# A short first tile, its own score buffers, filler transposes and new planned transfer times in a planned attention stage

## The chip, the cores and the metric

One core of a Trainium2 chip runs the whole program. The metric is the device time of one execution in microseconds (us). Five engines work side by side and meet at semaphores: TensorE (PE in the rows; PEld is its weight load), VectorE (DVE), ScalarE (ACT), GpSimd (POOL) and SyncE (SP), which here only issues DMAs. Transfers issued from SP and POOL are carried by the same 16 DMA engines; the rows call their busy time the DMA share.

## The reference

Three layers follow one another. The first is attention with mixed heads, for 4 batches, 12 heads, 448 positions and a head size of 64:

```python
scores = scale * np.matmul(q, k.transpose(0, 1, 3, 2))
scores = np.einsum('bhij,hg->bgij', scores, w_pre)
attn = np.exp(scores - np.max(scores, axis=-1, keepdims=True))
attn = attn / (np.sum(attn, axis=-1, keepdims=True) + 1e-09)
attn = np.einsum('bhij,hg->bgij', attn, w_post)
return np.matmul(attn, v)
```

Its output, 1792 tokens of 768, goes through a layer h = x @ w_in, h * cos(h), @ w_out (inner width 2048), and that through a soft mixture of 8 experts. w_in and w_out come as doubles (float64) and are turned to float32 by the kernel itself.

## The kernel before, in words

**Stages.** phase_a is the attention (to about 533 us), phase_b the middle layer (to about 850 us), phase_c the experts. Only phase_a is touched.

**Tiles and groups.** Each batch's 448 query rows are cut into four tiles, t = 0 to 3, of 120, 120, 120 and 90 rows (ROWS); in a 90-row tile 88 rows are new and two are loaded twice. The 16 tiles stand in the list `tiles`, batch by batch and t = 0, 1, 2, 3. A tile is worked off in groups of 30 rows: 4 groups, or 3 for t = 3 (NG), 60 in all. `gi` counts groups and `ti` tiles.

**Steps of a tile.**
- load_q (L253) loads its queries into qnat in three parts of four heads, each one DMA, or two for t = 3 (80 rows and 10 rows). load_k (L239) loads a batch's keys in two halves of four DMAs; load_v (L271) its values in three.
- k_prep (L283) and q_prep (L306) transpose them on TensorE into PSUM and split each into a high and a low part (kp, kr and qh, ql) on ScalarE and VectorE. There is one qh and one ql, so q_prep of a tile waits for the scores of the tile before.
- scores (L339) makes the scores of a pair of heads in six matmuls (L351). Each head is copied out (`out`, helper lines L223 for VectorE and L225 for ScalarE) to a buffer ss from the ring "ssrc" of 8 places, and a DMA, `sort` (L366), writes it to s2, where the 12 heads of one position stand in neighbouring partitions. The sort goes from SP's queue or POOL's. A place of the ring is free again when its sort has landed.
- pre (L393) mixes heads for a third of a group: a matmul with kron_pre, the maximum on VectorE (L396), the exponential on ScalarE (L400). It needs all 12 sorts of its tile. fin (L416 to L418) forms the weights wc, post (L431) mixes again, four quarters of three matmuls each, and copies the result into am[ti % 2], one of two buffers of [112, 12, 4, 120]. av (L455) multiplies with the values, and the result is stored.

**Doubles.** `narrow` (L493) turns 64 units of 128 x 384 doubles to float32: a load raw (SP), two ScalarE steps (L507, L511), four on VectorE (L515, L519, L524, L528), two on POOL (L532, L535), a store (L538).

**The order is planned.** Every step is an Op of a Plan, with a planned duration for each engine that may do it, dependencies, a due time counted in groups, and the buffers that it takes or uses. `Plan.schedule` plays the program through with these durations and at each turn takes, among the steps that could start first on an engine, the one that is due first. Its result is the fixed order of each engine's instructions; on the chip nothing is chosen again. A transfer is planned with the issuing engine's time and with `moves`, its time on the one planned wire, after which 3.5 us (SP) or 4.5 us (POOL) pass until it counts as seen, and `late` more for some. `behind` holds a step back until another has begun. The due times of a tile count back from its first group: scores S_DUE to S_DUE + S_SPAN before it, loads before these. The units of doubles are due evenly from group N_FIRST to N_LAST, their loads 1.5 groups sooner and behind the first pre product (`mixed`) of group int(due - 3).

PSUM has 8 banks: three of tag "ps", and in the first 24 takings also banks of the tags "pre" and "post" (SPARE), which have no other use at the start.

The costs of the plan that the change touches:

```python
kload[b, half, t] = dma(0.55, 0.8, start, due=due, ...
vload[b, c] = dma(0.35, 1.3, start, due=due, late=5.0, ...
    moves=0.85, behind=[sorted_[ti, 0]] if h else [])
ld = dma(0.4, 1.0, load, due=due - 1.5, late=6.0, takes=[raws], behind=behind)
```

Of the kernel before, what the change touches and what calls it, by code (L numbers as in the profile page):

```python
# [9 lines left out]
F32 = mybir.dt.float32  # L10
# [15 lines left out]
SPARE = 3 * ["ps", "pre", "ps", "pre", "ps", "post", "pre", "post"]  # L26

K_DUE, S_DUE, S_SPAN, P_DUE, AV_DUE, AV_SPAN, STAY = 4.0, 3.2, 3.6, 1.8, 0.7, 3.0, 0.4
N_FIRST, N_LAST = 3.5, 55.0
INV2PI = 1.0 / (2.0 * math.pi)  # L30

LEAST = 3.4332275390625e-05
# [144 lines left out]
def phase_a(tc, ident, q, k, v, w_pre, w_post, xT_d, wide, start_next):  # L177
    nc = tc.nc
    B, H, S, D = q.shape
# [6 lines left out]
    with ExitStack() as ctx:  # L186
# [23 lines left out]
        ql = sp.tile([128, H // 2, 120], F32R, name="q_lo")  # L210
        am = [sl.tile([CJ, H, NJ, 120], F32, name=f"am{i}") for i in range(2)]

        tiles = [(b, t) for b in range(B) for t in range(4)]
        groups = [(ti, g) for ti, (b, t) in enumerate(tiles) for g in range(NG[t])]
        NT, NGR = len(tiles), len(groups)
        first = [groups.index((ti, 0)) for ti in range(NT)]
# [15 lines left out]
        def dma(dur, moves, start, **kw):  # L232
            return plan.op([("SP", dur)], lambda e: start(), moves=moves, **kw)
# [5 lines left out]
        def load_k(b, half, t, due, behind):  # L239
            if t == 0:  # L240
                kslot[b, half] = Slot("knat")

            def start():
                if t == 0:
                    knat[b, half] = room(sp, "knat", [CJ, NJ, 6, D], F32, f"knat{b}_{half}")
                nc.sync.dma_start(
                    out=knat[b, half][:, t],
                    in_=k[b, 6 * half:6 * half + 6, t::NJ, :].rearrange("h p d -> p h d"))
            kload[b, half, t] = dma(0.55, 0.8, start, due=due, late=3.0 if b else 0.0, takes=[] if t else [kslot[b, half]],
                                    uses=[kslot[b, half]] if t else [],  # L250
                                    behind=behind + ([kload[b, half, 0]] if t else []))

        def load_q(ti, part, due, behind):  # L253
            b, t = tiles[ti]
            m = H // 3
            if part == 0:
                qslot[ti] = Slot("qnat")

            def start():
                if part == 0:  # L260
                    qnat[ti] = room(sp, "qnat", [120, H, D], F32, f"qnat{ti}")
                h = m * part
                for r, n, i in ((0, 80, 360), (80, 10, S - 10)) if t == 3 else ((0, 120, 120 * t),):
                    nc.sync.dma_start(
                        out=qnat[ti][r:r + n, h:h + m],
                        in_=q[b, h:h + m, i:i + n, :].rearrange("h i d -> i h d"))
            qload[ti, part] = dma(1.0 if t == 3 else 0.5, 0.55, start, due=due, late=3.0 if ti > 1 else 0.0, takes=[qslot[ti]] if part == 0 else [],
                                  uses=[] if part == 0 else [qslot[ti]],
                                  behind=behind + ([qload[ti, 0]] if part else []))

        def load_v(b, c, due, behind):  # L271
            def start():
                nc.sync.dma_start(
                    out=vt[:, 4 * c:4 * c + 4],
                    in_=v[b, 4 * c:4 * c + 4].rearrange("h (p t) d -> p h t d", t=NJ))
            vload[b, c] = dma(0.35, 1.3, start, due=due, late=5.0,
                              deps=[avs[4 * b - 1, c]] if b else [], behind=behind)


# [26 lines left out]
        def q_prep(ti, x, due):  # L306
            n = ROWS[tiles[ti][1]]
            s = Slot("ps")
            cs = slice(2 * x, 2 * x + 2)

            def src():
                return made["qt", ti, x][:, :240].rearrange("p (c i) -> p c i", c=2)[:, :, :n].rearrange(
                    "p c (a i) -> p c a i", i=10)

            def dst(to):

                return to[:, cs, :n].rearrange("p c (i a) -> p c a i", i=10)

            def turn(e):
                pt = made["qt", ti, x] = bank(s, f"qt{ti}_{x}")  # L320
                for c in range(2):
                    nc.tensor.transpose(
                        pt[:, c * 120:c * 120 + n],
                        qnat[ti][:n, 4 * x + 2 * c:4 * x + 2 * c + 2].rearrange("p h d -> p (h d)"),
                        ident[:n, :n])

            def high(e):
                copy(e, dst(qh), src())

            def low(e):  # L330
                nc.vector.tensor_tensor(out=dst(ql), in0=src(), in1=dst(qh).bitcast(F32), op=ALU.subtract)
            free = [qk[ti - 1, p] for p in (2 * x, 2 * x + 1)] if ti else []
            a = plan.op([("PE", 0.21)], turn, [qload[ti, x]] + free, due, takes=[s], uses=[qslot[ti]])
            h = plan.op([("ACT", 0.32), ("DVE", 0.5)], high, [a], due, uses=[s])
            qdone[ti, x] = plan.op([("DVE", 0.5)], low, [h], due, uses=[s])
# [3 lines left out]
        def scores(ti, p, due):  # L339
# [13 lines left out]

            def out(o):
                def f(e):
                    x[o] = room(sg, "ssrc", [120, S], F32, f"ss{ti}_{2 * p + o}")
                    copy(e, x[o][:n], made["s", ti, p][o][:n, :S])
                return f

# [8 lines left out]
            qk[ti, p] = plan.op([("PE", 0.8)], mul, [kdone[b, p], qdone[ti, p // 2]], due, takes=s, half=True)  # L368
            for o in range(2):
                h = 2 * p + o  # L370
                ss = Slot("ssrc")
                if h == 0:
                    s2l[ti] = Slot("s2")
                c = plan.op(EV, out(o), [qk[ti, p]], due, takes=[ss], uses=[s[o]])
                sorted_[ti, h] = plan.op([("SP", 1.0), ("POOL", 0.8)], sort(o), [c], due,
                                         takes=[] if h else [s2l[ti]], uses=[ss] + ([s2l[ti]] if h else []),
                                         moves=0.85, behind=[sorted_[ti, 0]] if h else [])


        el, et, mz, prt, wct, expd, wcl, mixed = {}, {}, {}, {}, {}, {}, {}, {}  # L380
# [43 lines left out]
        def post(gi, jt, f, due):  # L424
# [10 lines left out]
            def out(e):  # L435
# [1 line left out]
                     made["po", gi, jt][:, :360].rearrange("p (g i) -> p g i", i=30))  # L437
            m = plan.op([("PE", 0.63)], mul, [f], due, takes=[b], uses=[el[gi], wcl[gi]])
            amdone[gi, jt] = plan.op([("ACT", 0.36), ("DVE", 0.46)], out,
                                     [m] + ([avs[ti - 2, s] for s in range(3)] if ti > 1 else []), due, uses=[b])  # L440


        xst, xl = {}, {}
# [29 lines left out]
        def av(ti, due):  # L473
# [10 lines left out]
                outs.append(plan.op([("ACT", 0.28), ("DVE", 0.36)], lambda e, s=s: av_out(ti, s, e),  # L484
                                    [avs[ti, s]], d, uses=[sl_, xl[ti]]))
            if ti < NT - 2:
                dma(0.4, 1.25, lambda: store_x(ti, nc.sync), late=5.0, deps=outs, due=due + 2, uses=[xl[ti]])


        UP = 384  # L490
# [2 lines left out]
        def narrow(u, due, behind):  # L493
# [42 lines left out]

            def store():
                nc.sync.dma_start(out=dst[:, c0:c0 + UP], in_=x["f"])  # L538
            ld = dma(0.4, 1.0, load, due=due - 1.5, late=6.0, takes=[raws], behind=behind)
            m = plan.op([("ACT", 0.46)], size, [ld], due, takes=[ms], uses=[raws])  # L540
            f = plan.op([("ACT", 0.46)], rest, [ld], due, takes=[fs], uses=[raws])
            t = plan.op([("DVE", 0.42)], bits, [ld], due, takes=[ts], uses=[raws])
# [2 lines left out]
            p = plan.op([("DVE", 0.34)], power, [t], due, uses=[ts, ms])  # L545
            f = plan.op([("POOL", 1.05)], times, [p, f], due, uses=[fs, ms])
            f = plan.op([("POOL", 1.05)], plus, [f], due, uses=[fs, ts])
            dma(0.35, 0.55, store, late=6.0, deps=[f], due=due + 1, uses=[fs])


        for b in range(B):
            for ti in range(4 * b, 4 * b + 4):
                g0, n = first[ti], NG[tiles[ti][1]]
                mark = [qk[ti - 1, 0]] if ti > 2 else [qk[1, 5]] if ti > 1 else [kload[0, 1, 3]] if ti else []
                for p in range(6):
                    d = g0 - S_DUE - S_SPAN * (5 - p) / 5
                    if p % 2 == 0:
# [653 lines left out]
```

## Time and profile before

| what | us |
|---|---|
| median of 3 runs | 962.73 |
| lowest and highest of the 3 | 960.71, 968.0 |
| the profiled execution's own time | 964.6 |
| its span, from the first to the last instruction | 962.8 |
| TensorE busy in the span | 908.4 (94%) |
| VectorE, ScalarE, GpSimd busy | 658.8, 562.3, 198.4 |
| mean granted TensorE clock | 0.972 |

The profile is one execution. A group of rows tells busy time and idle time by line of the kernel; "idle before" names the event that ended an engine's wait, inferred from semaphores, so that a name may stand for another that came at the same time. PEclk is the granted clock of TensorE, 1.00 being 2.4 GHz and 0.50 being 1.2 GHz.

### The profile page before, as it was taken

To read this page: it belongs to the slowest core of one execution; us is meant where nothing else is said; L and a number is where in the kernel's file an instruction comes from. 1 tells how busy PE (TensorE), PEld (TensorE's weight loads), DVE (VectorE), ACT (ScalarE), POOL (GpSimd) and SP (SyncE) were. 2 spreads that over 40 slices of the span, in tenths; PEclk is the share of its full clock that TensorE was granted. 3 is DMA by queue.
4 is the path that set the end of the run, shared out by engine and by line. 5 is a ranking of instruction groups with operands and counts; after the bars stand their busy time and mean duration, and the time that the engine had idled before them with its cause. 6 is when DMAs were issued, how large, how long until landed. Compare 5 with 4: busy or idle time off the path is not lost.

```text
span 962.8 us, 18155 instructions
## 1 busy us (share of the span) xinstructions
PE 908.4 (94%) x6694; PEld 650.0 (68%) x6694; DVE 658.8 (68%) x1295; ACT 562.3 (58%) x1240; POOL 198.4 (21%) x246
## 2 busy tenths in 40 slices
PE   5888999999989999998999999999999999999985
PEld 3556677676767667766778877877777778844422
DVE  4578988979879789889854756666767667833303
ACT  4566776777767758766665645556657557720102
POOL 2144443524534245334410000000000000000000
PEclk9789999999999989999999999999999999999897
DMA  9989678996678985978427731254554438899999
GB/s 178 213 182 232 181 202 209 209 250 201 169 187 206 234 217 152 231 213 209 141 65 243 255 123 50 82 197 131 181 171 157 132 115 279 262 348 380 373 372 329
DMA packets 195246, 198.92 MB, mean 207 GB/s; under 512 B 71042, under 2 KB 164368, under 8 KB 195158
## 3 DMA queue, kind: packets, MB, share of 16 engines
q1 hardware_dynamic: 184626, 176.06, 62.5%
q0 software_dynamic: 7920, 21.05, 9.2%
q8 instruction: 53, 0.87, 0.4%
q10 hardware_dynamic: 2612, 0.65, 0.3%
q14 instruction: 35, 0.29, 0.1%
HBM read 135.40 MB, written 23.59 MB: 165 GB/s over the span
## 4 chain that ended last, share of the span: by engine, by line
PE 75%; DVE 9%; DMA 9%; ACT 3%; issue 2%; SPq 1%; POOL 0%; DVEq 0%; ACTq 0%
PE po L431 13%; PE pre L393 12%; PE h L698 8%; PE h L699 8%; PE h L701 8%; PE s L351 6%; PE av L455 6%; DMA early<-in_moe_w_dram 4%; DMA s<-ss 3%; PE gt L738 3%; DVE cvt L519 2%; PE lg L747 1%; PE eh L1018 1%; PE p L810 1%; DMA qnat<-in_q_dram 1%
## 5 line engine op out<-in xcount | busy, mean ns | idle before, releaser
L431 PEld LDWEIGHTS po<-wc,e 120*112 120x112 f32 x1440 | 174.8, 180 | 71.3 <-issue 45.5
L431 PE MATMUL po<-wc,e 120*112 120x120 f32 x1440 | 187.5, 272 | 7.0 <-ACT am L225 3.3
L393 PE MATMUL pre<-s,kron_pre 120*120 120x448 f32 x360 | 173.4, 567 | 9.0 <-DMA w<-nar 3.2
L698 PE MATMUL h<-x,wh 128*128 128x512 f32 (+1 forms) x384 | 142.1, 380 | 0.0
L400 ACT ACTIVATE e<-pre,mz 120x448 f32<-120x448 f32 x180 | 115.0, 639 | 43.3 <-DVE mz L396 42.9
L396 DVE TENSOR_REDUCE mz<-pre 120x1 f32<-120x448 f32 x180 | 111.0, 620 | 40.2 <-PE pre L393 39.6
L699 PE MATMUL h<-x,wh 128*128 128x512 f32 (+1 forms) x384 | 136.3, 365 | 0.0
L225 ACT COPY am<-po 112x360 f32<-112x360 f32 x191 | 87.4, 462 | 66.6 <-PE po L431 65.1
L366 POOL DMA_DIRECT2D s<-ss x104 | 63.5, 611 | 205.7 <-ACT ss L225 148.2
L714 ACT ACTIVATE cg<-h,consts 128x512 f32<-128x512 f32 (+1 forms) x64 | 40.4, 632 | 90.8 <-PE h L701 88.0
L698 PEld LDWEIGHTS h<-x,wh 128*128 128x128 f32 x384 | 72.3, 188 | 22.9 <-ACT cg L714 8.4
L701 PE MATMUL h<-x,wf 128*128 128x512 f32 (+1 forms) x384 | 87.5, 364 | 0.0
L455 PE MATMUL av<-am,v 112*64 112x120 f32 (+1 forms) x1536 | 83.5, 265 | 0.6 <-ACT ss L225 0.5
L455 PEld LDWEIGHTS av<-am,v 112*64 112x64 f32 x1536 | 74.9, 138 | 12.4 <-issue 3.4
L532 POOL TENSOR_TENSOR nar<-nar,cvm 128x384 f32<-128x384 f32 x64 | 64.4, 1006 | 88.5 <-DVE cvm L528 32.3
L715 DVE TENSOR_SCALAR cg<-cg 128x512 f32<-128x512 f32 (+1 forms) x64 | 25.2, 394 | 79.8 <-ACT cg L714 79.4
L699 PEld LDWEIGHTS h<-x,wh 128*128 128x128 f32 x384 | 72.4, 189 | 10.5
L1024 POOL MEMSET hz<- 128x256 f32 x2 | 0.6, 305 | 358.3 <-DVE rz L973 358.3
L701 PEld LDWEIGHTS h<-x,wf 128*128 128x128 f32 x384 | 66.3, 188 | 11.8
L225 ACT COPY ss<-s 120x448 f32<-120x448 f32 (+1 forms) x109 | 56.8, 534 | 28.2 <-PE s L351 18.1
L535 POOL TENSOR_TENSOR nar<-nar,cvt 128x384 f32<-128x384 f32 x64 | 68.4, 1068 | 4.2
L393 PEld LDWEIGHTS pre<-s,kron_pre 120*120 120x120 f32 x360 | 54.0, 190 | 22.0 <-issue 19.6
(178 smaller groups left out, 1468.2 us busy)
## 6 DMA issues: line engine op xcount, KB each, us to landing
early<-in_moe_w_dram SPq DMA_DIRECT2D x36, 768.0 KB
wf<-w SPq DMA_DIRECT2D x64, 384.0 KB
s<-ss POOLq DMA_DIRECT2D x79, 210.0 KB, 6.2
s<-ss SPq DMA_DIRECT2D x65, 210.0 KB
raw<-in_moe_w_in_dram SPq DMA_DIRECT2D x32, 384.0 KB
w<-nar SPq DMA_DIRECT2D x64, 192.0 KB
raw<-in_moe_w_out_dram SPq DMA_DIRECT2D x32, 384.0 KB
gn<-in_moe_w_dram SPq DMA_DIRECT2D x16, 768.0 KB
```

The costliest lines, as they stand in the source:

```text
L225: nc.scalar.copy(out=out, in_=in_)
L366: QUEUE[e].dma_start(out=s2t[ti][h::12, :n // 10], in_=x[o][:n])
L393: nc.tensor.matmul(prt[gi, c][:, :S], kpre, s2t[ti][:, 3 * g + c, :], start=True, stop=True)
L396: nc.vector.tensor_reduce(out=mz[gi][:, 0, c:c + 1], in_=prt[gi, c][:, :S], axis=AX.X, op=ALU.max, negate=True)
L400: nc.scalar.activation(out=et[gi][:, c, :], in_=prt.pop((gi, c))[:, :S], func=AF.Exp, bias=mz[gi][:, 0, c:c + 1], accum_out=mz[gi][:, 1, c ...
L431: nc.tensor.matmul(pt[:, :360].rearrange("p (g i) -> p g i", i=30)[:, :, 10 * c:10 * c + 10], et[gi][:, c, jt * CJ:(jt + 1) * CJ], wct[gi] ...
L455: nc.tensor.matmul(pt[64 * o:64 * o + 64, x * 120:x * 120 + n], vt[:, g, jt, :], am[ti % 2][:, g, jt, :n], start=(jt == 0), stop=(jt == NJ ...
L532: nc.gpsimd.tensor_tensor(out=x["f"], in0=x["f"], in1=x["m"], op=ALU.mult)
L535: nc.gpsimd.tensor_tensor(out=x["f"], in0=x["f"], in1=x["t"].bitcast(F32), op=ALU.add)
L698: nc.tensor.matmul(pt, wh[:, c], xh[:, c, :], start=(c == 0), stop=False)
L699: nc.tensor.matmul(pt, wh[:, c], xl[:, c, :], start=False, stop=False)
L701: nc.tensor.matmul(pt, wl[:, c], xh[:, c, :], start=False, stop=(c == 5))
```

## The change

Batch 0's tiles run in the order t = 3, 0, 1, 2, so that tile 0 has 90 rows and three groups, and all groups of batch 0 after it are numbered accordingly. Tile 0's twelve score copies go to twelve places cut from am[1], which tile 1's results use first, and take no place in the ring; tile 1's results wait for tile 0's sorts. The query turns of tile 1 are each preceded by 10, 8 and 8 transposes of the identity into an unused part of their bank. Tile 1's queries are loaded behind tile 0's third pair of scores, not behind the last key load. N_FIRST is 5.5, not 3.5. The planned times of most transfers are longer: a sort's `moves` 1.0 (0.75 for 90 rows) for 0.85, a key load's 0.9 for 0.8, a query part's 0.65 for 0.55, a value load's 1.9 for 1.3, a result's store 1.5 for 1.25, the load and the store of a unit of doubles 1.45 and 0.75 for 1.0 and 0.55.

```diff
-N_FIRST, N_LAST = 3.5, 55.0
+WARM = 10, 8, 8
+N_FIRST, N_LAST = 5.5, 55.0
...
-        tiles = [(b, t) for b in range(B) for t in range(4)]
+        tiles = [(b, t) for b in range(B) for t in ((3, 0, 1, 2) if b == 0 else (0, 1, 2, 3))]
...
-            kload[b, half, t] = dma(0.55, 0.8, start, due=due, late=3.0 if b else 0.0, takes=[] if t else [kslot[b, half]],
+            kload[b, half, t] = dma(0.55, 0.9, start, due=due, late=3.0 if b else 0.0, takes=[] if t else [kslot[b, half]],
...
-            qload[ti, part] = dma(1.0 if t == 3 else 0.5, 0.55, start, due=due, late=3.0 if ti > 1 else 0.0, takes=[qslot[ti]] if part == 0 else [],
+            qload[ti, part] = dma(1.0 if t == 3 else 0.5, 0.65, start, due=due, late=3.0 if ti > 1 else 0.0, takes=[qslot[ti]] if part == 0 else [],
...
-            vload[b, c] = dma(0.35, 1.3, start, due=due, late=5.0,
+            vload[b, c] = dma(0.55, 1.9, start, due=due, late=5.0,
...
             def turn(e):
                 pt = made["qt", ti, x] = bank(s, f"qt{ti}_{x}")
+                for _ in range(idle):
+                    nc.tensor.transpose(pt[:, 256:384], ident, ident)
...
             free = [qk[ti - 1, p] for p in (2 * x, 2 * x + 1)] if ti else []
+            idle = WARM[x] if ti == 1 else 0
...
             def out(o):
-                    x[o] = room(sg, "ssrc", [120, S], F32, f"ss{ti}_{2 * p + o}")
+                    if ti:
+                        x[o] = room(sg, "ssrc", [120, S], F32, f"ss{ti}_{2 * p + o}")
+                    else:
+                        c = S * (2 * p + o)
+                        x[o] = am[1].rearrange("p h t i -> p (h t i)")[:, c:c + S]
                     copy(e, x[o][:n], made["s", ti, p][o][:n, :S])
...
             qk[ti, p] = plan.op([("PE", 0.8)], mul, [kdone[b, p], qdone[ti, p // 2]], due, takes=s, half=True)
                 h = 2 * p + o
-                ss = Slot("ssrc")
+                ss = [Slot("ssrc")] if ti else []
                     s2l[ti] = Slot("s2")
-                c = plan.op(EV, out(o), [qk[ti, p]], due, takes=[ss], uses=[s[o]])
+                c = plan.op(EV, out(o), [qk[ti, p]], due, takes=ss, uses=[s[o]])
-                                         takes=[] if h else [s2l[ti]], uses=[ss] + ([s2l[ti]] if h else []),
-                                         moves=0.85, behind=[sorted_[ti, 0]] if h else [])
+                                         takes=[] if h else [s2l[ti]], uses=ss + ([s2l[ti]] if h else []),
+                                         moves=1.0 * n / 120, behind=[sorted_[ti, 0]] if h else [])
...
             m = plan.op([("PE", 0.63)], mul, [f], due, takes=[b], uses=[el[gi], wcl[gi]])
-                                     [m] + ([avs[ti - 2, s] for s in range(3)] if ti > 1 else []), due, uses=[b])
+                                     [m] + ([avs[ti - 2, s] for s in range(3)] if ti > 1 else [sorted_[0, h] for h in range(H)] if ti else []), due, uses=[b])
...
-                dma(0.4, 1.25, lambda: store_x(ti, nc.sync), late=5.0, deps=outs, due=due + 2, uses=[xl[ti]])
+                dma(0.4, 1.5, lambda: store_x(ti, nc.sync), late=5.0, deps=outs, due=due + 2, uses=[xl[ti]])
...
-            ld = dma(0.4, 1.0, load, due=due - 1.5, late=6.0, takes=[raws], behind=behind)
+            ld = dma(0.45, 1.45, load, due=due - 1.5, late=6.0, takes=[raws], behind=behind)
...
-            dma(0.35, 0.55, store, late=6.0, deps=[f], due=due + 1, uses=[fs])
+            dma(0.4, 0.75, store, late=6.0, deps=[f], due=due + 1, uses=[fs])
-                mark = [qk[ti - 1, 0]] if ti > 2 else [qk[1, 5]] if ti > 1 else [kload[0, 1, 3]] if ti else []
+                mark = [qk[ti - 1, 0]] if ti > 2 else [qk[1, 5]] if ti > 1 else [qk[0, 2]] if ti else []
```

## Rows read from the trace of the kernel before

**Rows 1.** Stages: window, us, busy by engine (instructions), granted clock, DMA share, GB/s.
```profile
0.00:100.00 100.00, 80.80 (x490) 52.79 (x492) 63.55 (x134) 58.07 (x142) 31.13 (x46) 0.90 0.93 204
100.00:490.00 390.00, 375.45 (x3158) 273.74 (x3154) 332.94 (x666) 273.01 (x703) 164.42 (x191) 0.98 0.77 198
...
533.00:850.00 317.00, 315.44 (x1857) 246.04 (x1856) 210.99 (x392) 193.60 (x310) 0.00 (x0) 1.00 0.52 166
```

**Rows 2.** The same view of the start; busy are PE, PEld, DVE, ACT, POOL.
```profile
0.00:30.90 30.90, 17.82 (x96) 11.74 (x96) 11.13 (x23) 13.32 (x26) 7.22 (x17) 0.86 0.88 179
30.90:36.20 5.30, 5.30 (x9) 2.46 (x9) 2.45 (x5) 1.79 (x5) 0.58 (x1) 0.52 0.73 176
36.20:57.30 21.10, 17.59 (x110) 12.14 (x108) 15.66 (x37) 15.45 (x40) 5.36 (x6) 0.98 1.07 244
57.30:64.00 6.70, 6.65 (x16) 2.92 (x18) 3.05 (x6) 2.68 (x7) 0.62 (x1) 0.55 0.56 107
64.00:92.20 28.20, 25.69 (x208) 18.09 (x206) 25.36 (x53) 19.82 (x51) 14.69 (x18) 1.00 1.01 223
```

**Rows 3.** Timeline of the start: start, us, engine, line, operation [idle before, releaser].
```profile
12.03 0.72 POOL L366 DMA_DIRECT2D s<-ss  x1 [10.72 <-ACT ss L225]
...
21.42 0.62 DVE L223 COPY ss<-s 120x448 f32<-120x448 f32 x1 [3.19 <-DMA s<-ss]
21.60 0.58 POOL L366 DMA_DIRECT2D s<-ss  x1 [1.83 <-ACT ss L225]
...
25.20 0.66 PE L322 MATMUL qt<-ident,qnat 120*128 120x120 f32 x2 [6.05 <-ACT ss L225]
...
30.92 0.47 PEld L393 LDWEIGHTS pre<-s,kron_pre 120*120 120x120 f32 x2 [0.56 <-DMA s<-ss]
```

**Rows 4.** Windows of the idle stretch and of what follows it.
```profile
19.20:25.20 6.00, 0.00 (x1) 0.00 (x1) 0.62 (x1) 1.12 (x3) 1.15 (x2) 0.76 0.91 180
25.20:30.90 5.70, 4.17 (x14) 2.14 (x14) 1.48 (x3) 1.68 (x4) 1.74 (x3) 0.50 0.72 182
```

**Rows 5.** Timeline where tiles 1 and 2 open, and a late sort of tile 1.
```profile
46.77 0.58 POOL L366 DMA_DIRECT2D s<-ss  x1 [5.26 <-ACT ss L225]
...
57.35 1.82 PE L393 MATMUL pre<-s,kron_pre 120*120 120x448 f32 x2 [3.15 <-DMA w<-nar]
...
92.26 0.98 PE L393 MATMUL pre<-s,kron_pre 120*120 120x448 f32 x2 [1.95 <-DMA s<-ss]
```

**Rows 6.** DMA issues, 100 to 490 us: count, size, median us to landing.
```profile
s<-ss POOLq DMA_DIRECT2D x57, 210.0 KB, 6.1
...
s<-ss POOLq DMA_DIRECT2D x21, 157.5 KB, 3.6
```

**Rows 7.** Timeline of TensorE: twelve key transposes in a row.
```profile
12.80 1.37 PE L289 MATMUL kt<-ident,knat 112*128 112x112 f32 x12
```

**Rows 8.** Windows of the score products alone (L351): PE, PEld busy.
```profile
0.00:19.20 19.20, 7.47 (x48) 5.03 (x48) 1.00 0.91 178
```

**Rows 9.** Chain of waits: one third of a group's pre, one quarter of its post.
```profile
42.20 0.75 PE pre L393 x2
42.95 0.61 PE po L431 x6
```

**Rows 10.** VectorE's conversion groups, 100 to 490 us; last: least, median, longest ns.
```profile
L519 DVE SCALAR_TENSOR_TENSOR cvt<-raw,cvt 128x384 uint32<-128x384 uint32 x56 | 49.1, 877 | 1.0
...
L524 DVE SCALAR_TENSOR_TENSOR cvt<-cvm,cvt 128x384 f32<-128x384 f32 x56 | 35.9, 641 | 1.7 <-ACT cvm L507 0.5
...
L515 DVE TENSOR_SCALAR cvt<-raw 128x384 uint32<-128x384 uint32 x56 | 27.1, 484 | 2.3 <-DMA raw<-in_moe_w_out_dram 2.3
...
L528 DVE TENSOR_SCALAR cvm<-cvt 128x384 uint32<-128x384 uint32 x56 | 19.8, 354 | 0.8
...
L519 DVE SCALAR_TENSOR_TENSOR cvt<-raw,cvt x64: 540/560/2128, 47.7 to 475.1; 128x384 uint32<-128x384 uint32 x64
```

**Rows 11.** A window later on in which a batch changes.
```profile
340.00:350.00 10.00, 7.92 (x32) 5.45 (x33) 7.28 (x12) 5.16 (x13) 5.07 (x6) 0.66 0.92 232
```

## The prediction

> **What bounds the kernel now.** I read the busy times by stage first. The attention stage, to 533 us, has 499 us of TensorE work; from 100 to 490 us TensorE is busy 375.5 of 390 us, and from 533 to 850 us 315.4 of 317 [rows 1]. So a change confined to the attention's plan can only take out its idle and half-clock time. Of that the first 100 us hold most: 19.2 us idle and a mean granted clock of 0.90, where the next 390 us hold 14.5 us and 0.98 [rows 1].
>
> Next, the start in stretches [rows 2]. Up to 30.9 us TensorE works 17.8 us. From 30.9 to 36.2 it is busy without a break at a mean clock of 0.52, and 57.3 to 64 is alike at 0.55. The DMA share is 0.88 and 1.07 ahead of these two. So the start waits for transfers, and pays again in the clock.
>
> The timeline tells which transfers [rows 3]. Tile 0's first sorting transfer leaves at 12.03 us. Its scores go out by eight rotating ss buffers, so the copies of the last heads wait for earlier sorts to land: one starts at 21.42 after 3.19 us of idle that "DMA s<-ss" ended, and a sort behind such a copy leaves at 21.60. TensorE stands still for 6.05 us before 25.20, and the first pre product starts at 30.92, released by a sort. In that hole the granted clock falls: its mean from 19.2 to 25.2 us is 0.76, and from 25.2 to 30.9 it is 0.50, the lower of its two levels, 1.2 GHz [rows 4].
>
> Two more holes follow. The pre product at 57.35 had 3.15 us of idle before it and the one at 92.26 1.95 [rows 5]; both open a new tile. The view names a store of converted weights for the first, but that store has no reader there; I take the real releaser to be tile 1's last sort, which leaves only at 46.77, because the late scores wait for buffers too.
>
> **The change, part by part.** Terms are differences on the profiled execution.
>
> (a) *Short tile first, twelve own buffers.* The first pre needs tile 0's twelve sorts. Now each carries 157.5 KB, not 210, and no copy waits for a landing, so the last head's copy, which follows its product, can come near 18 us. The wire then decides: 12 x 157.5 KB = 1.94 MB plus 0.37 MB of tile 1's queries is 2.30 MB. The start ran at 179 GB/s, with 176 to 244 in the stretches beside it [rows 2]; at 195 the 2.30 MB take 11.8 us. From the first sort at 12.03, with 0.4 us more (tile 0's query parts are two DMAs each, and the first keys queue on SP behind one of them) and 1.3 us until the last packets are seen, this ends near 25.5 us, 5.4 us before 30.92. Bounds: at 244 GB/s with no extra 21.5 us, which 1.9 us to land makes 23.4; at 179 and the full size 29.8. So -7.5 to -1.1; I take **-5.4**.
>
> A rule speaks against the size. By the Trainium skill (SBUF — State Buffer, Door 1: The DMA port swizzle) a transfer's rate hangs on the ports that its partitions reach; partitions 0 to 89 leave eight partitions on each of the eight busiest ports, as 0 to 119 do, so a 90-row sort would take a 120-row sort's time. The trace speaks against it: from 100 to 490 us POOL's sorts of 210 KB land in 6.1 us, those of 157.5 KB in 3.6 [rows 6], though at different loads.
>
> (b) *Clock and fillers.* The stretch 30.9 to 36.2 loses 5.3 x 0.48 = 2.5 us to the clock [rows 2]. Before the first pre the changed order has tile 1's first four pairs, as before, and 26 more transposes. At the twelve key transposes' 1.37 us [rows 7], and 128 columns for 112, they take 26 x 0.114 x 1.14 = 3.4 us. TensorE stopped at 19.15 with eight pairs of scores done, 0.93 us each, six of them tile 0's [rows 8], so tile 0's end near 17.3; four pairs of tile 1 add some 3.2 at the later ones' 0.8, and TensorE is at work until 23.9 of 25.5, so the transposes hide, with 1.6 us to spare; without that cover they cost up to 3.4. I expect the clock to stay up: **-2.5** (0 to -2.5, and +3.4 if the fillers do not hide).
>
> (c) *The hole at tile 1.* It costs 3.5 us idle (21.1 less 17.59) and 6.7 x 0.45 = 3.0 us of clock [rows 2]. Tile 1 now finds eight unused ss buffers, so its last two pairs need only the first landings, near 29 us instead of 39 and 45. The loads of doubles, six of which (2.4 MB) ran between 32 and 53 us, begin behind the third group's first product. Against it, tile 0 covers three groups, not four: a group is 3 pre of 0.75 and 4 po of 0.61 us [rows 9], 4.7 us, and needs the sorts at 25.5 + 14.1 + the two pairs and query turns, about 43. Wire: 1.94 + 0.37 + 2.58 MB at 200 GB/s from 12.4 end at 37, seen near 39; the values (1.38 MB), if in front, make it 46. Half the hole goes: **-3.5** (0 to -6.5; +3 if it deepens, a rival below).
>
> (d) *The hole at tile 2*: 64 to 92.2 us holds 2.5 us of idle [rows 2], 1.95 of it there. Four or five conversions are loaded ahead of it instead of eight, but its tile comes a group sooner: **-1.0** (0 to -2.5).
>
> (e) *Later queries of tile 1.* Their three issues move on SP behind tile 0's third pair of scores, among the sorts; at some 0.5 us each they delay a sort and tile 1's transposes, which have the 1.6 us of (b). With the two-part query loads: **+0.4** (0 to +1.5).
>
> (f) *Denser conversions.* 64 units in 49.5 groups instead of 51.5 push 2/0.817 = 2.4 units behind the start, 2.36 us of VectorE each (484 + 877 + 641 + 354 ns) [rows 10], 5.8 us in all. VectorE is 85% busy there, TensorE idle 3.7% [rows 1]. Hidden wholly it costs 0, not at all 5.8; nearer the first: **+1.5**.
>
> The Trainium skill (SBUF — State Buffer, Who interferes with whom) says that a VectorE instruction with two SBUF inputs and a GpSimd one that reads SBUF lock each other out of a shared port. The mean of 877 ns for L519 agrees: its median is 560 and its longest 2128 [rows 10]. By it, each deferred unit brings more of this; the full 5.8 us is then the price.
>
> (g) *New planned times* only reorder. The old ones let a 393 KB load of doubles take 1.0 us, 393 GB/s, where these stretches moved at most 244 [rows 2]; the new 1.45 us is 271. Products behind a transfer are thus placed later, ready ones ahead of them. What can be won are later holes, such as 340 to 350 us with 2.1 us idle and 3.4 of clock [rows 11]. Every order makes new ones, though: **-1.0** (-8 to +8).
>
> Sum: -5.4 - 2.5 - 3.5 - 1.0 + 0.4 + 1.5 - 1.0 = -11.5. On the profiled 964.6 us this is 953.1; that execution lay 1.9 above the median of 962.7, so **951.2**.
>
> **Rivals.** *The wire takes it back at tile 1.* Cover is one group shorter, the first pre 5.4 us earlier, so the sorts are wanted 10 us sooner than before; if the values stand ahead of them, the hole stays and grows by 3 us. For it: DMA shares of 1.07 and 1.01 up to 92 us [rows 2]. Against it: no doubles are in front. -5.4 - 2.5 + 3.0 + 0.4 + 1.5 = -3.0, so 959.7.
>
> *VectorE takes over after 100 us* (the other side). The full 5.8 us of (f) stand on the path, and crowded conversions hold po's weights back, each time with an idle spell and a clock drop as at 340 to 350 us (5.5 us) [rows 11]: two more are 11.0. -11.5 - 1.5 + 5.8 + 11.0 = +3.8, so 966.5. It decides once VectorE gets past some 95% busy in a stretch of tens of us; the 85% speak against it.
>
> *The short sort saves no wire time.* At the old size the 0.65 MB saved cost 3.3 us of (a): 954.5. This is the port rule's case; rows 6 speak against it.
>
> *Truer times clear the later holes as well*: (g) at its -8, 944.2. For it: the 14.5 us of idle and, at a clock of 0.98, some 8 us lost to it [rows 1]. Against: of 22 us only what waits for transfers can go, and the wire's share stays 0.77.
>
> That the change does nothing at the start is hardly open: the buffers are plainly apart, and the waits that go are the ones in rows 3.
>
> **How the numbers follow.** Forecast, 946 to 957: 0.48. Wire at tile 1: 0.24. VectorE: 0.10. No wire saved: 0.09. Later holes cleared: 0.09. A measurement of this kernel can tell about 1%, 9.6 us, from no change: the line is at 953.1. The forecast lies below it about 7 times in 10 (0.33), with the cleared holes 0.09 and a third of the third rival 0.03: in all faster 0.46, when 0.01 is added for the wire's case going better. Slower than 972.4 needs VectorE's case with one more such hole, or a bad order of its like: 0.06. Within 1%: 0.48. The range, 941 to 965, takes in the wire's case and stops short of VectorE's.
>
> **What would show it.** Right: first pre near 25.5 us with no score copy of tile 0 released by a sort; granted clock 1.00 from 20 to 38 us; the fourth group's first pre with under 2 us of idle; no load of doubles before 35 us. Wrong: a first pre after 28 us (wire), a half-clock stretch after it (fillers), an idle spell over 4 us where tile 1 opens (cover), VectorE over 90% from 100 to 490 us, or more idle there than 14.5 us (order).

## The result and the profile after

The changed kernel takes 947.8 us (median of 4, 945.6 to 949.8); its ratio to the kernel before is 0.985, with a 95% interval of 0.981 to 0.990. The forecast was 951.2 in a range of 941 to 965. The profiled execution has a span of 945.4 us, against 962.8.

First where the gain lies. The middle layer's first product (L698 before, L710 after) starts at 530.7 us before and at 512.9 after, and from there to the end both take the same, 432.1 and 432.5 us. The attention stage gained 17.8 us, and what it gains goes into the time undiminished. Some 3 to 4 us of the 17.8 belong to the one execution of the kernel before that was profiled: it took 964.6 us, and by the ratio of 0.985 the gain is some 14 us.

The table gives the time at which TensorE has done the weighted products (po, 24 records per group) of so many groups, counted from the trace record by record:

| groups done | before, us | after, us | lead, us |
|---|---|---|---|
| 2 | 49.28 | 42.28 | 7.00 |
| 4 | 69.17 | 69.26 | -0.09 |
| 8 | 106.35 | 100.51 | 5.83 |
| 16 | 170.46 | 166.19 | 4.27 |
| 20 | 203.67 | 197.38 | 6.29 |
| 27 | 263.96 | 257.51 | 6.45 |
| 30 | 291.64 | 281.42 | 10.22 |
| 36 | 335.95 | 326.51 | 9.43 |
| 37 | 351.82 | 336.44 | 15.38 |
| 47 | 432.72 | 418.42 | 14.30 |
| 49 | 452.92 | 435.88 | 17.04 |
| 58 | 515.38 | 497.74 | 17.64 |

Single rows swing by some us, because the two orders put other work between these products. Some 6 us of the lead are there when the start is over. The larger part comes in four later steps, the largest of them near 340 us, where nothing in the diff points. The stages of the kernel after, by window (columns as in [rows 1]):

```profile
0.00:100.00 100.00, 84.34 (x575) 58.06 (x576) 63.93 (x132) 59.73 (x144) 26.02 (x41) 0.97 0.92 193
100.00:490.00 390.00, 382.58 (x3265) 279.71 (x3265) 345.55 (x685) 283.25 (x729) 168.15 (x193) 1.00 0.78 202
```

Against [rows 1], TensorE's idle time from 100 to 490 us falls from 14.5 to 7.4 us, and the granted clock there rises from 0.98 to 1.00. VectorE is busier in the same stretch, 345.5 us for 332.9.

The start of the kernel after, in windows and in TensorE's timeline:

```profile
20.00:30.00 10.00, 9.09 (x56) 5.85 (x56) 5.20 (x9) 4.17 (x9) 2.33 (x4) 1.00 0.83 203
...
40.00:50.00 10.00, 8.89 (x52) 5.71 (x52) 6.45 (x16) 6.25 (x16) 1.04 (x2) 1.00 1.12 232
...
60.00:70.00 10.00, 6.22 (x24) 4.16 (x25) 3.15 (x7) 4.64 (x11) 3.74 (x5) 0.66 0.89 175
```

```profile
18.09 1.31 PE L326 MATMUL qt<-ident 128*128 128x128 f32 x10
...
27.88 2.52 PE L405 MATMUL pre<-s,kron_pre 120*120 120x448 f32 x6
...
43.38 0.98 PE L405 MATMUL pre<-s,kron_pre 120*120 120x448 f32 x2 [1.11 <-issue]
...
63.78 1.16 PE L358 MATMUL s<-k_hi,q_hi 64*120 64x448 f32 x2 [4.30 <-ACT ss L228]
```

The first pre product starts at 27.88 us, not 30.92 [rows 3], and its six matmuls follow in 0.42 us each: TensorE worked through the wait, fillers among it, and the clock is 1.00 where it was 0.50 [rows 4]. The hole where tile 1 opens shrank from 3.15 us [rows 5] to 1.11, with no drop of the clock after it. A new one stands where tile 2's scores are made, at 63.78: a copy waits 4.8 us for a place, TensorE for the copy, and the clock falls to a mean of 0.66. What stands around it on SP's queue, and the link before it in the chain of waits, are these:

```profile
42.81 8.57 SPq L249 DMA_DIRECT2D knat<-in_k_dram  x3
51.70 0.79 SPq L378 DMA_DIRECT2D s<-ss  x1
52.54 0.49 SPq L249 DMA_DIRECT2D knat<-in_k_dram  x1
53.08 1.19 SPq L267 DMA_DIRECT2D qnat<-in_q_dram  x1
54.31 8.84 SPq L249 DMA_DIRECT2D knat<-in_k_dram  x3
63.26 0.86 SPq L378 DMA_DIRECT2D s<-ss  x1
```

```profile
51.70 11.40 DMA s<-ss
```

A sort issued at 51.70 lands 11.4 us later, and the copy follows it. Around this sort SP issues the next batch's eight key loads, three of which take 8.8 us to issue.

Later on, the windows that answer to [rows 11] and its like:

```profile
180.00:200.00 20.00, 19.87 (x144) 14.12 (x146) 16.55 (x33) 14.37 (x38) 6.39 (x9) 1.00 1.05 220
...
270.00:290.00 20.00, 20.00 (x168) 14.90 (x167) 17.89 (x37) 14.84 (x38) 9.04 (x10) 1.00 0.75 209
...
340.00:350.00 10.00, 9.94 (x65) 6.42 (x65) 9.70 (x22) 9.04 (x24) 3.25 (x4) 1.00 0.59 200
...
440.00:450.00 10.00, 10.00 (x90) 7.13 (x90) 7.39 (x17) 7.37 (x21) 3.20 (x4) 1.00 0.80 229
```

Before, the same four windows were:

```profile
180.00:200.00 20.00, 17.84 (x143) 13.15 (x139) 14.82 (x25) 10.92 (x30) 7.98 (x9) 0.91 1.12 235
270.00:290.00 20.00, 16.96 (x143) 13.16 (x142) 13.89 (x27) 11.84 (x30) 8.68 (x10) 0.91 0.70 156
...
440.00:450.00 10.00, 6.96 (x62) 4.51 (x61) 9.72 (x17) 5.53 (x14) 6.23 (x8) 1.00 0.77 196
```

With 340 to 350 from [rows 11] they held 2.2 + 3.0 + 2.1 + 3.0 = 10.3 us of idle and 1.8 + 1.8 + 3.4 = 7.0 us lost to the clock (window length times the missing share). After, they hold 0.2 us and nothing.

### The profile page after: what moved, and what is told of

It is laid out like the page before. It is cut to its first block, busy times and chain, and to the rows that moved or that the text cites. A ratio compares the mean times of both kernels' runs of the same rounds, so it can differ in the third digit from the quotient of the medians.

```text
span 945.4 us, 18209 instructions
## 1 busy us (share of the span) xinstructions
PE 901.4 (95%) x6720; PEld 648.5 (69%) x6720; DVE 663.4 (70%) x1294; ACT 563.6 (60%) x1241; POOL 196.5 (21%) x242
## 4 chain that ended last, share of the span: by engine, by line
PE 73%; DVE 12%; DMA 7%; ACT 3%; issue 3%; SPq 1%; DVEq 0%; ACTq 0%
PE po L443 11%; PE pre L405 10%; PE h L710 8%; PE h L711 8%; PE h L713 8%; PE av L467 5%; PE s L358 5%; PE gt L750 3%; DMA early<-in_moe_w_dram 3%; PE eh L1030 2%; DMA s<-ss 2%; DVE cvt L531 2%; DVE mz L408 2%; PE etr L1039 2%; PE lg L759 2%
## 5 line engine op out<-in xcount | busy, mean ns | idle before, releaser
L443 PEld LDWEIGHTS po<-wc,e 120*112 120x112 f32 x1440 | 171.8, 177 | 63.8 <-issue 41.7
L443 PE MATMUL po<-wc,e 120*112 120x120 f32 x1440 | 184.7, 270 | 2.3 <-ACT am L228 1.0
L405 PE MATMUL pre<-s,kron_pre 120*120 120x448 f32 x360 | 166.5, 550 | 5.2 <-ACT e L412 2.7
L710 PE MATMUL h<-x,wh 128*128 128x512 f32 (+1 forms) x384 | 142.0, 380 | 0.0
L228 ACT COPY am<-po 112x360 f32<-112x360 f32 x184 | 84.6, 464 | 50.7 <-PE po L443 49.2
L378 POOL DMA_DIRECT2D s<-ss x93 | 56.4, 607 | 178.6 <-ACT ss L228 106.4
L710 PEld LDWEIGHTS h<-x,wh 128*128 128x128 f32 x384 | 72.2, 188 | 23.0 <-ACT cg L726 8.0
L655 DVE TENSOR_TENSOR wf<-wf,wh 128x768 fp32r<-128x768 f32 x64 | 60.9, 952 | 9.9 <-ACT wh L654 9.9
```

What stands on the lines that cost most here:

```text
L228: nc.scalar.copy(out=out, in_=in_)
L405: nc.tensor.matmul(prt[gi, c][:, :S], kpre, s2t[ti][:, 3 * g + c, :], start=True, stop=True)
L443: nc.tensor.matmul(pt[:, :360].rearrange("p (g i) -> p g i", i=30)[:, :, 10 * c:10 * c + 10], et[gi][:, c, jt * CJ:(jt + 1) * CJ], wct[gi] ...
L655: nc.vector.tensor_tensor(out=wf_t[v], in0=wf_t[v].bitcast(F32), in1=wh.bitcast(F32), op=ALU.subtract)
L710: nc.tensor.matmul(pt, wh[:, c], xh[:, c, :], start=(c == 0), stop=False)
```

## Experiments

Two questions: which part of the change gave the 17.8 us, and is the better order after 100 us the work of truer planned times, or just another order? In the table, "products" is the start of the middle layer's first product in the profiled execution, "idle" is 390 us less TensorE's busy time from 100 to 490 us there. The kernel before, measured beside each set, had medians of 960.8 to 962.5 us there. Medians are set side by side across sets where they differ by several us; the ratios carry the intervals.

| run | median, us | ratio to before, 95% interval | products, us | idle, us |
|---|---|---|---|---|
| changed kernel | 947.8 | 0.985 (0.981 to 0.990) | 512.9 | 7.4 |
| only_times | 952.6 | 0.990 (0.987 to 0.994) | 518.4 | 9.7 |
| old_times | 953.4 | 0.992 (0.989 to 0.996) | 515.4 | 10.4 |
| no_filler | 950.5 | 0.989 (0.985 to 0.994) | 514.6 | 7.7 |
| early_doubles | 949.0 | 0.987 (0.983 to 0.992) | 512.9 | 10.1 |
| ring | 946.3 | 0.985 (0.980 to 0.989) | 512.5 | 9.5 |
| before_nudged | 958.3 | 0.995 (0.992 to 0.998) | 518.4 | 12.4 |
| nudged | 956.6 | 0.996 (0.993 to 0.998) | 522.7 | 13.0 |
| nudged_down | 952.2 | 0.989 (0.984 to 0.994) | 520.4 | 10.7 |
| only_times_nudged | 957.5 | 0.997 (0.994 to 0.999) | 522.9 | 13.9 |
| late_keys | 939.8 | 0.976 (0.972 to 0.981) | 507.4 | 4.7 |
| late_keys_nudged | 942.7 | 0.981 (0.977 to 0.985) | 513.4 | 10.2 |
| before_late_keys | 954.9 | 0.993 (0.991 to 0.996) | 526.9 | 11.2 |

From "products" to the end of the span every one of these takes 431.6 to 433.0 us: all differences arise in the attention stage. "products" and "idle" are of one execution, which can lie some us off the median: that of before_nudged took 953.2 us, that of late_keys_nudged 947.8.

### The planned times alone, and everything else alone

only_times is the kernel before with the seven new planned times (two of the lines):

```diff
-                                         moves=0.85, behind=[sorted_[ti, 0]] if h else [])
+                                         moves=1.0 * n / 120, behind=[sorted_[ti, 0]] if h else [])
...
-            ld = dma(0.4, 1.0, load, due=due - 1.5, late=6.0, takes=[raws], behind=behind)
+            ld = dma(0.45, 1.45, load, due=due - 1.5, late=6.0, takes=[raws], behind=behind)
```

> The kernel before with the new planned transfer times alone; start, buffers, fillers and N_FIRST are as before. Theory (the planned times give most of it): the order after 100 us is the better one, idle time of TensorE from 100 to 490 us falls from 14.5 us to 8 or less and the clock there rises to 1.00, and the ratio to before is 0.983 to 0.990 (10 to 16 us), though the first pre product still starts near 31 us. Rival (the parts at the start give it): the ratio is 0.997 to 1.003. Rival (any new order moves the time by chance): anywhere from 0.985 to 1.01.

old_times is the changed kernel with these lines the other way round.

> The changed kernel with the old planned transfer times; the short first tile, its own buffers, the fillers and N_FIRST of 5.5 stay. Theory (planned times): the first pre product still comes near 28 us, but holes at the batches' ends come back and the ratio to before is 0.993 to 0.999 (1 to 7 us, the start's share). Rival (the start gives it): 0.982 to 0.988. Rival (chance): anywhere from 0.985 to 1.01.

Each alone gains half to two thirds: 0.990 and 0.992, where both together have 0.985. Both ratios lie just outside what the theory expected, and both lie in the range for chance, which is too wide to exclude much; only_times' idle time fell to 9.7 us and not to 8, though its clock after 100 us is 1.00. What tells more is that old_times, with the old planned times, also lost most of the late holes. This is old_times' window from 100 to 490 us, in the same columns:

```profile
100.00:490.00 390.00, 379.64 (x3236) 278.08 (x3234) 339.41 (x681) 281.26 (x722) 167.32 (x192) 1.00 0.77 201
```

The clock is 1.00 there too. At the 37th group, where the kernel before lost the most, old_times raises its lead from 5.6 to 11.8 us. So truer times aren't needed to lose that hole; a different order is enough. The start shows the other side. In only_times the first pre comes at 29.84 us, after the same kind of hole as before, and slowly (4.28 us for six matmuls at a mean clock of 0.58, TensorE's timeline of only_times):

```profile
29.84 4.28 PE L393 MATMUL pre<-s,kron_pre 120*120 120x448 f32 x6 [0.24 <-DMA s<-ss]
```

### What a new order is worth by itself

before_nudged and nudged move one planned time, the sort's, by 2 and 3%:

```diff
-                                         moves=0.85, behind=[sorted_[ti, 0]] if h else [])
+                                         moves=0.87, behind=[sorted_[ti, 0]] if h else [])
```

> The kernel before with one planned time moved by 2%: a sort's 0.85 is 0.87; nothing else. It asks what a new order is worth by itself. Theory (the new planned times are nearer to what transfers take, and that is what pays): the ratio to before is 0.997 to 1.005, the hole near 340 us may move, idle time from 100 to 490 us stays within 3 us of 14.5 and some stretch there still falls to the lower clock. Rival (the order before is an unlucky one, and any other is better): 0.985 to 0.994, with 6 us or more of the idle and clock loss after 100 us gone.

```diff
-                                         moves=1.0 * n / 120, behind=[sorted_[ti, 0]] if h else [])
+                                         moves=1.03 * n / 120, behind=[sorted_[ti, 0]] if h else [])
```

> The changed kernel with a sort's planned time 3% longer still (1.03 for 1.0). Theory (truer times pay): within 2 us of the changed kernel. Rival (luck of the order): it moves by 4 us or more either way, with holes of 2 us or more at other places after 100 us.

nudged_down has 0.97 in the same place; only_times_nudged is only_times with 1.03.

> The changed kernel with a sort's planned time 3% shorter (0.97). If the order is a matter of luck: some other time between 943 and 958, with holes of 2 us or more at places of its own. If 1.0 is the true time and both sides lose: 953 or more. If only too long a time loses: within 2 us of 947.8.

> The kernel before with the new planned times, the sort's 3% longer still. If the new times pay for themselves: below 956, as the 952.6 without the 3%. If that was one order's luck: 956 to 963.

A step of 3% in one number costs the changed kernel 8.8 us, more than half of its gain; its interval (0.993 to 0.998) does not meet the changed kernel's. 3% the other way stands between at 952.2, its interval overlapping that of the changed kernel; it is not within 2 us of 947.8, as it would be if only too long a time lost. only_times loses 4.9 us by the same step, to 957.5, on the side that was to show one order's luck, though the two intervals touch. The kernel before gains some 2 to 5 us by its own step; 0.995 falls between the two cases that were set for it. Of the 9.8 us that its profiled execution lies behind the changed kernel's at the 58th group, 5.9 are there by the eighth: tile 2's hole is larger. The rest comes later, with 2.6 us of idle at 308.7. TensorE's timeline of nudged and its windows:

```profile
71.20 0.73 PE L358 MATMUL s<-k_hi,q_hi 64*120 64x448 f32 x2 [7.22 <-DVE ss L226]
76.44 1.54 PE L443 MATMUL po<-wc,e 120*112 120x120 f32 x6 [2.29 <-ACT am L228]
```

```profile
100.00:490.00 390.00, 376.96 (x3198) 274.67 (x3197) 350.61 (x694) 280.85 (x722) 171.82 (x197) 1.00 0.79 204
...
70.00:80.00 10.00, 6.51 (x24) 4.24 (x26) 8.55 (x15) 4.14 (x11) 5.40 (x6) 0.50 0.84 238
```

So the rival "luck of the order" stands. With the whole change, three orders have the ratios 0.985, 0.989 and 0.996, mean 0.990; with the new times alone 0.990 and 0.997; with neither 1 and 0.995. On these few orders the change as a whole is worth some 7 us (means of 0.998 and 0.990), and the order that it happened to get some 4 more. Whether the planned times by themselves are worth anything isn't settled: without the changes at the start the means differ by some 4 us (0.998 and 0.994), with them old_times' one order (0.992) lies some 2 us above the mean of three.

Not all of the late gain is one order's luck, though. Two of the four late holes of the kernel before, the ones near 189 and 278 us, stand in two other orders too that have the old times and the old start: in before_nudged, and in before_late_keys (below). TensorE's timelines of the two:

```profile
183.73 0.87 PE L431 MATMUL po<-wc,e 120*112 120x120 f32 x6 [2.14 <-ACT am L225]
273.28 1.30 PE L393 MATMUL pre<-s,kron_pre 120*120 120x448 f32 x2 [2.88 <-DMA w<-nar]
```

```profile
193.13 0.87 PE L431 MATMUL po<-wc,e 120*112 120x120 f32 x6 [2.17 <-ACT am L225]
281.54 1.82 PE L393 MATMUL pre<-s,kron_pre 120*120 120x448 f32 x2 [3.36 <-DMA s<-ss]
```

From 170 to 300 us TensorE is idle for 6.3, 7.1 and 7.2 us in these three kernels, and for 1.4 to 3.6 us in the eleven that have the new times, the new start or both. Either part was thus enough to lose these two holes, the start alone in the one order of old_times; how it does so isn't shown. From 300 to 490 us there is no such line between them: 3.8 to 7.0 us in the three, 1.7 to 7.6 in the others.

### The parts at the start

no_filler, early_doubles and ring each take one part out of the changed kernel. No run takes out the short tile alone, or the later queries of tile 1 alone. First no_filler:

```diff
-WARM = 10, 8, 8
+WARM = 0, 0, 0
```

> The changed kernel without the 26 filler transposes. If they hold the clock: the granted clock falls to 0.50 somewhere between 22 and 36 us, the first products after it take twice as long, and the time is 2 to 4 us above the changed kernel. If they do not matter: clock 1.00 to 60 us without them too, the pre products start up to 1.5 us sooner, and the time is the changed kernel's within 1.5 us.

The clock does fall without the fillers, and the first six pre matmuls take 4.19 us for 2.52 (a window and TensorE's timeline of no_filler):

```profile
20.00:30.00 10.00, 7.40 (x24) 3.93 (x25) 2.68 (x5) 2.38 (x5) 2.19 (x4) 0.59 0.81 198
```

```profile
28.62 4.19 PE L405 MATMUL pre<-s,kron_pre 120*120 120x448 f32 x6 [0.55 <-DMA s<-am]
```

The time is 2.7 us above the changed kernel's, as expected, but within both intervals. The mechanism is shown by the clock; its price in the end isn't told apart from none.

```diff
-N_FIRST, N_LAST = 5.5, 55.0
+N_FIRST, N_LAST = 3.5, 55.0
```

> The changed kernel with N_FIRST back at 3.5. If the early loads of doubles hold up the sorts: two or three more of them are issued before 60 us, tile 1 and tile 2 open 2 to 6 us later and the time is 2 to 6 us above the changed kernel. If they are hidden: within 2 us of it, or better, since the conversions are less dense later.

949.0 us is within the 2 us. Two more loads of doubles are issued before 60 us, and the first products of tiles 1 and 2 come later, at 47.34 us for 43.38 and at 87.41 for 85.07, as in the first case; but the time doesn't follow. The seventh group is even done 6.7 us sooner than in the changed kernel, and the middle layer starts at the same 512.9 us. What N_FIRST does for the sorts was not what mattered.

In ring, tile 0's copies take places of the ring again:

```diff
-                    if ti:
+                    if True:
                         x[o] = room(sg, "ssrc", [120, S], F32, f"ss{ti}_{2 * p + o}")
...
-                ss = [Slot("ssrc")] if ti else []
+                ss = [Slot("ssrc")]
...
-                                     [m] + ([avs[ti - 2, s] for s in range(3)] if ti > 1 else [sorted_[0, h] for h in range(H)] if ti else []), due, uses=[b])
+                                     [m] + ([avs[ti - 2, s] for s in range(3)] if ti > 1 else []), due, uses=[b])
```

> The changed kernel with tile 0's scores back in the ring of eight buffers; the short tile is still first. Theory (the wait for landings is what the own buffers remove): copies of the last heads are again released by a sort, the last sort of tile 0 leaves some 3 us later and the first pre product starts 2 to 4 us after 27.9; at the end the time is 1 to 4 us above the changed kernel. Rival (the wire alone sets the first pre): it starts within 1 us of 27.9 and the time is within 1.5 us.

The theory falls, and the rival (the wire alone sets the first pre) holds in both of its numbers. A copy is released by a landing again, but only 0.50 us late. Tile 0's last sort leaves 1.7 us later than in the changed kernel (20.81 for 19.13), and still the first pre starts 0.3 us sooner (timeline of ring):

```profile
18.24 0.53 ACT L228 COPY ss<-s 90x448 f32<-90x448 f32 x1 [0.50 <-DMA s<-ss]
...
27.60 2.49 PE L405 MATMUL pre<-s,kron_pre 120*120 120x448 f32 x6 [0.39 <-DMA s<-ss]
```

At 946.3 us the own buffers give nothing that can be seen. With the short tile first, the ring's waits are small.

### The next batch's keys

The new hole at tile 2 has the next batch's key loads around it on SP's queue. late_keys holds them back by one tile:

```diff
-                            load_k(b, p // 3, t, d - K_DUE - 2, [qk[4 * b - 2, 0]] if b else [])
+                            load_k(b, p // 3, t, d - K_DUE - 2, [qk[4 * b - 1, 0]] if b else [])
```

> The changed kernel with the key loads of a new batch held behind the last tile's first scores instead of the one before it. Theory (the hole of 60 to 70 us, in which tile 2's sort of 51.7 us lands only at 63.1, comes from batch 1's eight key loads between it on SP and on the wire): no key load before 60 us, tile 2's sorts land within 8 us, idle time from 60 to 70 us falls from 3.8 us to under 1 and its clock from 0.66 to 1.00, and the time is 3 to 6 us below the changed kernel, if the later loads do not open a hole near the batch's end. Rival (the wire is full in any case): tile 2 opens as late as now, within 2 us, and the time is within 2 us.

The time falls to 939.8 us; all its executions (937.3 to 941.8) lie below the changed kernel's (945.6 to 949.8). The key loads leave at 70 us, all eight in 10.1 us (SP's queue of late_keys), and in its windows the hole is smaller:

```profile
70.24 10.09 SPq L249 DMA_DIRECT2D knat<-in_k_dram  x8
```

```profile
100.00:490.00 390.00, 385.30 (x3295) 282.74 (x3294) 345.96 (x693) 283.38 (x729) 165.87 (x192) 1.00 0.79 206
...
60.00:70.00 10.00, 7.41 (x63) 5.35 (x60) 7.71 (x14) 6.14 (x17) 4.75 (x5) 0.94 0.81 198
```

But the details missed. Idle time from 60 to 70 us is 2.6 us, not under 1, and POOL's sorts issued from 40 to 66 us land in 8.8 us as in the changed kernel (8.9): five loads of doubles stand where the keys stood. So that the keys made the hole isn't shown. The lead over the changed kernel, counted as in the table of groups, is 1.0 us at the eighth group, 3.9 at the 25th, 4.6 at the 40th and 5.5 at the 58th, as at the first product of the middle layer. It isn't one hole that went. Two more runs ask whether this was luck as well: late_keys with the sort at 1.03, and the late keys on the kernel before.

> Late keys and the sort's planned time 3% longer together. Theory (late keys remove a wait, whatever the order): 8 us or more below the nudged kernel's 956.6, thus 948 or less, with no hole over 4 us between 60 and 80 us. Rival (the 939.8 of the late keys was a lucky order): within 4 us of 956.6, or a hole as large as before opens elsewhere before 100 us.

> The kernel before with the late keys alone. Theory (early keys of the next batch crowd SP and the wire where a tile's sorts are due, in any order): 4 to 12 us below before, 951 to 959, with first products of tiles 1 and 2 earlier than 57.4 and 92.3 us. Rival (it helps only where the first tile is short): within 3 us of before.

Late keys win with each of the three orders tried: 939.8 against 947.8, 942.7 against 956.6, 954.9 against some 961 to 962. The second has no hole over 4 us from 60 to 80 us, as expected. The third does not gain where it was expected: its tiles 1 and 2 open at 60.81 and 97.36 us, later than 57.35 and 92.26 [rows 5]. In its trace the gain comes after 325 us, but that execution took 961.0 us, 6 above its median, so the place is uncertain. Each of the three is also a new order, so luck isn't excluded; three gains of 6 to 14 us make it unlikely. By which wait late keys help is open.

## Why the prediction came out right, point by point

The total was right, 951.2 forecast and 947.8 measured, but by two errors that cancel, and so by luck. The start was to give 12.0 us in terms (a) to (e), and the rest to lose 0.5 in (f) and (g). Measured, the lead is 5.8 us at the eighth group, and the other 12.0 of the 17.8 us come later. Terms (a) to (d) as measured below make -6.2, close to the lead at the eighth group.

(a) -5.4 forecast, -3.0 measured: the first pre at 27.88 us and not 25.5, inside the bounds. The wire did decide, as the working has it, but its time was sized too small. Tile 0's last sort leaves SP at 19.13 us and, by the semaphore events of the trace after, lands at 27.67; TensorE comes to the first pre 0.2 us later, straight from a fifth pair of tile 1's scores (four were assumed). In no_filler, where TensorE waits there, such a sort plainly ends the wait at 28.48. The window from the first sort to the last landing in the trace after, and the chain of waits in no_filler:

```profile
12.40:27.70 15.30, 13.81 (x102) 9.27 (x98) 8.70 (x15) 8.89 (x18) 6.43 (x11) 1.00 0.76 182
```

```profile
18.10 10.38 DMA s<-am
```

In these 15.3 us the engines moved 2.79 MB at 182 GB/s, where the sum has 2.30 MB at 195 in 11.8 us. It leaves out tile 1's own sorts, eight of which leave from 22.10 to 27.35 us. The 0.49 MB more are some 2.7 us at 182 GB/s and the lower rate some 0.8 us, both estimates; the 1.3 us allowed for the last packets, behind which no row stands, cover a part. That tile 1's sorts delay tile 0's wasn't tested by itself. ring shows that the own buffers had no share. The port rule of the Trainium skill (SBUF — State Buffer, Door 1: The DMA port swizzle) was not tested by itself. Sorts of 157.5 KB land in 4.3 us in the trace after (19 of POOL, 100 to 490 us) and those of 210 KB in 5.8, a smaller difference than [rows 6] but the same way.

(b) -2.5: right. The clock is 1.00 from 10 to 60 us, the fillers lie in the wait (1.31, 1.09 and 1.04 us, for the 3.4 estimated), and no_filler shows the drop. What it is worth in the whole time isn't shown, as said above.

(c) -3.5 forecast; 1.1 us of a hole of 6.5 are left, so -5.4. The tile opens at 43.38 us, as the working had it (about 43).

(d) -1.0 was the wrong sign. The hole at tile 2 is 3.8 us idle and 3.4 us of clock in 60 to 70 us, against 2.5 of idle: +4.7. The step that failed is the account of what stands in front of tile 2's sorts: it counted conversions and left out the next batch's eight key loads (1.4 MB), which are issued between 42.8 and 64.7 us. How much of the hole is theirs is open, since without them, in late_keys, 2.6 us of idle are left. The rival "the wire takes it back" named the right kind of event, one tile too early.

(e) Its +0.4 can't be read apart. Tile 0's second half of keys leaves 1.9 us later than before (6.34 for 4.48), behind a part of queries that is now two loads, and tile 0's score products start 0.4 us later (10.09 for 9.68).

(f) +1.5: the bound of 5.8 did not come about. VectorE's busy share from 100 to 490 us rose to 89% (345.5 of 390), and TensorE's idle time fell all the same. VectorE's rival is out, at 89% where 95 was its point.

(g) -1.0 in a range of -8 to +8: this is the term that was mis-sized, and beyond its bound. 7.1 us of idle and 7.0 of clock went, and (f) and (g) together gave 12.0 us by the table of groups. The reason given ("products behind a transfer are placed later") isn't what the runs show: with the old times in old_times most of it goes too, and a 3% step brings a part back in another place. The rival "truer times clear the later holes" has a sum of the right size, but its cause isn't shown: the new times were enough to lose two of the holes, and so were the changes at the start without them, in one order.

## What to carry to other kernels

Where a greedy planner writes the order, a small step in any planned number gives another order, and here that alone moved the time by 3 to 9 us, as much as most parts of the change. So a part's worth is read from several orders with and without it, not from one pair; and a forecast of such a change needs a term for it that is as wide. Luck of the order is not a reason to stop looking, either: a hole that stays in several orders, as those near 189 and 278 us did, belongs to the plan. When a hole at the start is closed, look for which transfers meet the next tile's in SP's queue: here they belonged to the next batch, and holding them back gave 6 to 14 us in three orders, by a wait that is still open.

## What the runs showed that I had not expected

Everything behind the attention stage took 431.6 to 433.0 us in all fourteen kernels, whatever came before it. Key loads of 168 KB that SP issues in about 0.6 us each at the start (four in 2.36 us) took up to 4.3 us to issue at 47 us, with a DMA share of 1.12 in that stretch; the sorts that SP issues next leave behind them, such as the one at 51.70 us. And idle time does not follow the time closely: no_filler has 7.7 us of it after 100 us and takes 950.5, ring 9.5 and 946.3, since what an order saves there it may have lost before 100 us.
